# Convolution and token mixer on one core: y^T's last channels on both partition halves, a narrow identity among the first loads, the last batch's stores in halves, and a planner that knows the store queue and shifts due times by kind

## The chip, the cores and the metric

The kernel runs on one core of one Trainium2 chip. The metric is device time in microseconds for the whole program: inputs and output lie in HBM. Before the change the median of three runs is 185.41 us (185.27 to 186.28). The core has TensorE (PE, with its weight loads shown as PEld), VectorE (DVE), ScalarE (ACT), GpSimd (POOL) and SyncE (SP). Here GpSimd issues the loads of x (they convert float32 to bf16 on the way) and SyncE issues the weights' loads and all stores.

## The reference

x is 8 batches of 4,224 rows by 192 channels. First a causal convolution with 7 taps, whose weights are a softmax and are shared by the 24 channels of each of 8 heads. Then a mixer over the tokens of a batch.

```
y      = conv(x, softmax(weight))                 # per head of 24 channels, 7 taps
W_tok  = (y @ w_q) @ (y @ w_k).T / sqrt(64)       # 4224 x 4224 per batch
out    = relu(W_tok @ y) @ w_out                  # 192 x 192 output weights
```

The kernel never forms W_tok. Since W_tok y = (y w_q)(w_k^T y^T y) / 8, it computes G = y^T y (192 x 192) and M = w_k^T G (64 x 192), and then relu((y w_q) M) w_out.

## The kernel before, in words

**Tiling.** A batch is cut into 35 chunks of CW = 122 output rows (each is read as 128 input rows), and for the later steps into NSB = 5 blocks: four of 1,024 columns of y^T (two halves of 512) and one of 128. The loads of x come in groups of 18 chunks (of 9 in batch 0), whose edge chunks are separate transfers.

**Set-up.** GpSimd issues the first loads of x, then makes a wide identity (IDENTW, 128 x 128 x 4, an affine_select at L341), and ScalarE copies a narrow one (IDENT) from it (L363). VectorE computes the softmax (L349 to L373) and 14 products of the identity with tap weights (L392), TensorE adds them up (L405), ScalarE copies the sums into the banded convolution matrices (L416). ScalarE also zeroes the lower half of YTH in eight pieces (L432). SyncE issues the nine weight loads (L498) once the third group of x has landed, and nine casts on ScalarE (L503) make them bf16.

**A batch.** The functions add operations to a list, batch by batch:
- gen_conv: matmuls of two heads each (L553); the evacuation to Y goes to ScalarE or VectorE (L573).
- gen_transpose: for 8 chunks at a time, transposes of channels 0 to 127 into one PSUM bank (tr_lo, L594) and of channels 128 to 191 into another (tr_hi, L606), the second with two chunks side by side in two column halves of the array. VectorE copies the first to YTL (L616). The second needs two copies to YTH, one for each half of the partitions (L627), because YTH holds all 4,224 columns on partitions 0 to 63; partitions 64 to 127 stay zero, and so does the lower half of the weight WQH.
- gen_wq: the query projection of a block, WQL by YTL (L649) and WQH by YTH (L653), two column halves side by side, evacuated to WQT (L668).
- gen_gram: G, 6 chunks at a time, in column halves (L684), in a bank of its own.
- gen_mix_weights: G is copied (L703), transposed in part (L711), multiplied to M (L730), scaled on ScalarE (L749).
- gen_mix, for the batch before: M by WQT (L778 with row halves, L789), relu (L801, L802), the output projection (L828 with row halves, L846), evacuation to OUT (L862) and one store per block (L869; 768 KB, and 96 KB for the small block).

**What sets the order.** Planner.plan places all operations on the engines with estimated durations and latencies. Each operation has a due time vt in units of batches; among those that are ready on an engine the smallest vt wins, with STAY = 0.8 added on TensorE when an operation needs another array mode (128x128, 128x64, 64x128) than the one before. Loads have an expected landing time (op.lands), 0.26 us a chunk. The order that results is fixed: each engine runs its list in order and waits on semaphores. Seven PSUM banks are handed out by the same planner, the eighth is G's. Y and WQT have two buffers, YTL and YTH one, RT three, OUT four.

Of the kernel before, what the change touches and what calls it, by code (L numbers as in the profile page):

```python
# [14 lines left out]
class Op:  # L15
# [4 lines left out]
    def __init__(self, engines, emit, ns, needs=(), after=(), banks=0, drains=None, vt=0.0, mode=FULL, tail=0.0):  # L20
        self.engines = (engines,) if isinstance(engines, str) else tuple(engines)
        self.emit = emit

        self.ns = ns

        self.needs = [x for x in needs if x is not None]

        self.after = [x for x in after if x is not None]
        self.banks = banks

        self.drains = drains
# [8 lines left out]
        self.lands = 0.0  # L40
        Op.n += 1
        self.id = Op.n


class Planner:
# [8 lines left out]
    HOLD = 1.0  # L54

    def __init__(self, nbank, first_bank):
# [5 lines left out]
        self.bank_users = [[] for _ in range(nbank)]  # L62

# [19 lines left out]
    def plan(self):  # L83
# [9 lines left out]
        while left:  # L93
# [32 lines left out]
            free[e] = op.end  # L126
            if op.banks:
# [21 lines left out]
        return max(op.end for op in self.order)  # L149
# [66 lines left out]
def bass_lightweight_conv__then__hypermixer_token_mlp_kernel(  # L216
# [55 lines left out]
    ZERO = sbuf("zero", [128, 1], BF16)  # L272
# [4 lines left out]
    WQH = sbuf("wqh", [128, DH], BF16)  # L277
# [10 lines left out]
    YTH = sbuf("yth", [128, S], BF16)  # L288
# [17 lines left out]
    def add(*a, dma=None, **k):  # L306
        op = Op(*a, **k)
        op.dma = dma
        return planner.add(op)

    def evac_ns(cols, fast=1):
# [15 lines left out]
    one = add("DVE", lambda e, op: e.memset(IDENTW[:, :, :], 1.0), 350, vt=-9)  # L327
    zero_z = add("DVE", lambda e, op: e.memset(ZERO[:, :], 0.0), 80, vt=-8.95)
# [3 lines left out]
    zero_q = add("DVE", lambda e, op: e.memset(WQH[64:128, :], 0.0), 100, vt=-8.6)  # L332
# [6 lines left out]
    identw = add(  # L339
        "POOL",  # L340
        lambda e, op: e.affine_select(  # L341
            IDENTW[:, :, :], IDENTW[:, :, :], [[-1, 128], [0, HB]], ALU.is_equal, 0.0, base=0, channel_multiplier=1
        ),
        1600,
        needs=[one],
        vt=-3.85,
    )
# [13 lines left out]
    ident = add(  # L361
        "ACT",
        lambda e, op: e.copy(IDENT[:, :], IDENTW[:, :, 0]),  # L363
        170,
        needs=[identw],
        after=[ex],
        vt=-9,
    )
# [15 lines left out]
    band_done = []  # L384
    for f in range(2):
        fill, acc = None, None
        for k in range(KC):
            o = (f * KC + k) * CW * HB
            part = PARTS[:, o : o + CW * HB]
            made = add(  # L390
                "DVE",
                lambda e, op, part=part, k=k, f=f: e.tensor_tensor(  # L392
                    part.rearrange("p (j h) -> p j h", h=HB),
                    IDENTW[:, k : k + CW, :],
                    WSB[:, k, HB * f : HB * f + HB].unsqueeze(1).to_broadcast([128, CW, HB]),
                    ALU.mult,
                ),
                330,
                needs=[wn, identw],
                vt=-7 + f + 0.1 * k,  # L400
            )

            def collect(e, op, part=part, k=k, fill=fill):
                to = op if fill is None else fill
                return e.matmul(  # L405
                    bank(to.bank)[:, 0 : CW * HB], IDENT[:, :], part, start=k == 0, stop=k == KC - 1, skip_group_check=True
# [3 lines left out]
                "PE", collect, CW * HB / 2.4, needs=[made, ident], after=[acc], banks=1 if k == 0 else 0, vt=-7 + f + 0.1 * k  # L410
            )
            fill = fill or acc
        band_done.append(
            add(
                "ACT",
                lambda e, op, f=f, fill=fill: e.copy(  # L416
                    BAND[:, HB * f : HB * f + HB, 0:CW],
                    bank(fill.bank)[:, 0 : CW * HB].rearrange("p (j h) -> p h j", h=HB),
                ),
                56 + CW * HB / 1.2,  # L420
                needs=[acc],
                drains=fill,
                vt=-7 + f,
            )
        )
    zero_yt = []
    for i in range(8):
        n = S // 8
        zero_yt.append(
            add(  # L430
                "ACT",
                lambda e, op, i=i, n=n: e.copy(YTH[64:128, i * n : i * n + n], ZERO[64:128, 0:1].to_broadcast([64, n])),  # L432
                50 + n / 1.2,
                needs=[zero_z],
                after=band_done,
                vt=0.3 + 0.1 * i,
            )
        )
    out_first = [acc]
# [3 lines left out]
    at = [5200.0]  # L443

    def gen_load(b, gi):
# [23 lines left out]
        def emit(e, op):  # L469
            return [(e.dma_start(d, s), 16) for d, s in parts]  # L470

        at[0] += len(cs) * 260.0
        op = add(
            "POOL",
            emit,
            900 * len(parts),
            needs=[zero_x] if cs[-1] == NCC - 1 else [],
            dma=(f"x{b}_{gi}", sem, 16 * len(parts)),
            vt=-4 + b + gi * 0.1,
        )  # L480
        op.tail = 1500.0
        op.lands = at[0]
        load[b, gi] = op
# [16 lines left out]
    load_c = add("SP", emit_weights, 5000, needs=[load[0, 2]], dma=("c", S_C, 16 * 9), tail=2500, vt=-3)  # L500
# [4 lines left out]
    def twice(ap):  # L505
# [4 lines left out]
        cast(WQH[0:HI, :], WHI[0:HI, QS], [zero_q]),  # L510
# [15 lines left out]
    yt_done, yt_read, wq_read, rt_read, m_read = {}, {}, {}, {}, {}  # L526
# [11 lines left out]
    def gen_conv(b, gi):  # L538
# [6 lines left out]
        for hp in range(H // 2):  # L545
            vt = b + c0 / NCC - 0.15 + 0.02 * hp

            def conv(e, op, hp=hp):
# [15 lines left out]
                "PE", conv, mm_ns(n * GRP, 2), needs=[load[b, gi], band_done[hp // (HB // 2)], zero_b, zero_x, zero_x0], after=ev_needs, banks=nb, vt=vt  # L564
            )
# [9 lines left out]
            ev = add(both, evac, evac_ns(2 * n * GRP), needs=ev_needs, drains=mm, vt=vt)  # L575
# [3 lines left out]
    def gen_transpose(b, cs):  # L579
# [4 lines left out]
        half = (n + 1) // 2  # L584
# [12 lines left out]
        def tr_hi(e, op):  # L597
            ps = bank(op.bank).bitcast(BF16)
            last = None
            for k in range(half):  # L600
                for i in range(2):
                    if k + i * half >= n:
                        continue
                    c = cs[k + i * half]
                    w = width[c]
                    last = e.transpose(  # L606
                        ps[64 * i : 64 * i + HI, k * CW : k * CW + w], Y[0:w, yb, c, LO:D], IDENT[0:w, 0:w]
                    )
            return last

        mm_l = add("PE", tr_lo, 57 * n, needs=needs, after=free, banks=1, vt=vt)
        mm_h = add("PE", tr_hi, 57 * half, needs=needs, after=free, banks=1, vt=vt, mode=COL2)
# [4 lines left out]
                evac_ns(cols, 2), needs=free, drains=mm_l, vt=vt,  # L617
            )
        ]
        for i in range(2):  # L620
            a, z = t0 + i * half * CW, min(t1, t0 + (i + 1) * half * CW)
            if z <= a:
                continue
            evs.append(
                add(
                    "DVE",
                    lambda e, op, i=i, a=a, z=z: e.tensor_copy(  # L627
                        YTH[0:HI, a:z], bank(mm_h.bank).bitcast(BF16)[64 * i : 64 * i + HI, 0 : z - a]
                    ),
                    evac_ns(z - a, 2), needs=free, drains=mm_h, vt=vt,  # L630
                )
            )
        y_read.setdefault((b, "all"), []).extend([mm_l, mm_h])
        for c in cs:
            yt_done[b, c] = evs

    def gen_wq(b, j):
# [5 lines left out]
        wfree = wq_read.get((b - 2, j), [])  # L643

# [302 lines left out]
```

## Time and profile before

| | |
|---|---|
| Median of the runs | 185.41 us |
| Profiled execution | 185.54 us, of which 183.8 us span |
| TensorE busy | 163.0 us (89% of the span) |
| VectorE busy | 138.8 us (75%) |
| ScalarE busy | 127.5 us (69%) |
| GpSimd busy | 31.6 us (17%) |
| Bytes moved | 40.26 MB; 27.56 MB read from HBM, 25.95 MB written |

The span is that of the profiled execution, from its first to its last instruction. A group's row gives line, engine, operation, what is written from what, the count, and behind the bar busy microseconds and mean nanoseconds of one; behind the second bar the idle time before it and what ended it. TensorE's matmuls overlap, and their ends are modelled, so that the busy share is an upper bound of how full the engine is; the spacing of their starts tells more. A row of the timeline merges neighbouring instructions of one kind: start, length, engine, line, operation, and the count at the end.

### The profile page before, as it was taken

What the parts mean: (1) busy time and instruction counts of PE and PEld (TensorE: products, weight loads), DVE (VectorE), ACT (ScalarE), POOL (GpSimd) and SP (SyncE); (2) the same over time, 40 slices, a digit from 0 to 9 for tenths busy, and PEclk for the clock granted to TensorE, in tenths of its full rate; (3) what the DMA queues carried; (4) which work ended last, traced back from release to release, by engine and by line L of the source; (5) the groups of instructions that cost most, each with busy time, mean ns of one, the idle gap of its engine ahead of it and who ended that gap; (6) DMA issues with size and microseconds to landing.
All of it is one profiled execution on the core that took longest, in us unless ns stands there. A gap on an engine that the chain in (4) does not pass through costs nothing.

```text
span 183.8 us, 5487 instructions
## 1 busy us (share of the span) xinstructions
PE 163.0 (89%) x2390; PEld 108.7 (59%) x2390; DVE 138.8 (75%) x255; ACT 127.5 (69%) x220; POOL 31.6 (17%) x39
## 2 busy tenths in 40 slices
PE   0589869999999999999999999999999999979930
PEld 0248727666747575757566566677674856744520
DVE  6978868987678768877788796987679597768540
ACT  3079385778796868676784868787877786679730
POOL 7999923325030000000000000000000000000000
PEclk9999999999999999999999999999999999999996
DMA  3999999999999999999999952708442380844894
GB/s 24 182 186 189 202 193 191 191 194 192 322 288 236 266 277 294 266 277 215 335 280 282 247 213 92 277 5 341 165 170 107 126 318 25 342 175 180 328 385 180
DMA packets 47063, 40.26 MB, mean 219 GB/s; under 512 B 37568, under 2 KB 38848, under 8 KB 47040
## 3 DMA queue, kind: packets, MB, share of 16 engines
q0 software_dynamic: 36128, 13.61, 62.1%
q1 hardware_dynamic: 10912, 26.31, 38.9%
q8 instruction: 19, 0.31, 0.7%
q14 instruction: 4, 0.03, 0.0%
HBM read 27.56 MB, written 25.95 MB: 291 GB/s over the span
## 4 chain that ended last, share of the span: by engine, by line
PE 72%; DMA 7%; DVE 7%; ACT 4%; SPq 2%; POOL 2%; issue 2%; POOLq 0%
PE ps L846 15%; PE ps L684 12%; PE ps L553 9%; PE ps L828 9%; PE ps L594 7%; PE ps L649 5%; DMA xw<-in_x_dram 4%; PE ps L606 4%; PE ps L653 4%; PE ps L789 4%; PE ps L778 3%; DMA whi<-in_moe_w_out_dram 3%; SPq L498 2%; DVE rt L802 2%; DVE yth L627 2%
## 5 line engine op out<-in xcount | busy, mean ns | idle before, releaser
L862 ACT COPY out_sb<-ps 128x768 f32<-128x768 f32 (+1 forms) x43 | 33.1, 777 | 12.9 <-PE ps L846 12.3
L801 ACT ACTIVATE rt<-ps 128x1024 bf16<-128x1024 f32 (+3 forms) x49 | 33.1, 701 | 11.2 <-PE ps L778 10.7
L573 ACT CAST y<-ps 122x816 bf16<-122x816 f32 (+3 forms) x48 | 36.8, 795 | 4.7 <-PE ps L553 4.4
L862 DVE COPY out_sb<-ps 128x768 f32<-128x768 f32 (+1 forms) x29 | 24.1, 832 | 17.6 <-PE ps L846 17.5
L627 DVE COPY yth<-ps 64x488 bf16<-64x488 bf16 (+1 forms) x80 | 29.9, 374 | 6.6 <-PE ps L606 4.2
L684 PE MATMUL ps<-y 122*64 122x192 bf16 (+2 forms) x840 | 33.8, 221 | 0.4 <-issue 0.4
L470 POOL DMA_DIRECT2D xw<-in_x_dram x34 | 29.8, 904 | 22.9 <-issue 22.0
L553 PE MATMUL ps<-xw,band 128*128 128x432 bf16 (+3 forms) x144 | 30.3, 322 | 1.4 <-DVE y L573 0.5
L684 PEld LDWEIGHTS ps<-y 122*64 122x64 bf16 x840 | 28.5, 111 | 4.8 <-issue 3.8
L846 PE MATMUL ps<-wol,rt 128*128 128x192 bf16 x264 | 31.0, 251 | 0.0
L802 DVE TENSOR_SCALAR rt<-ps 128x512 bf16<-128x512 f32 (+2 forms) x31 | 25.3, 828 | 4.9 <-PE ps L789 3.7
L846 PEld LDWEIGHTS ps<-wol,rt 128*128 128x128 bf16 x264 | 21.0, 116 | 7.8 <-issue 2.1
L573 DVE CAST y<-ps 122x864 bf16<-122x864 f32 (+3 forms) x24 | 21.2, 902 | 3.3 <-PE ps L553 2.9
L616 DVE COPY ytl<-ps 128x976 bf16<-128x976 bf16 (+1 forms) x40 | 22.6, 589 | 1.2 <-PE ps L594 1.1
L828 PE MATMUL ps<-woh,rt 64*128 64x192 bf16 x264 | 21.0, 253 | 2.6 <-DVE rt L802 1.8
L594 PE MATMUL ps<-ident,y 122*128 122x122 bf16 x280 | 20.2, 216 | 1.4 <-DVE y L573 0.9
L594 PEld LDWEIGHTS ps<-ident,y 122*128 122x128 bf16 x280 | 16.8, 97 | 6.1 <-DVE y L573 1.1
L828 PEld LDWEIGHTS ps<-woh,rt 64*128 64x128 bf16 x264 | 10.4, 116 | 12.9 <-DVE rt L802 2.6
L553 PEld LDWEIGHTS ps<-xw,band 128*128 128x128 bf16 x144 | 11.6, 97 | 10.8 <-issue 2.4
L649 PE MATMUL ps<-ytl,wql 128*64 128x512 bf16 (+1 forms) x72 | 14.7, 373 | 1.3 <-ACT y L573 1.1
L606 PE MATMUL ps<-ident,y 122*64 122x122 bf16 x280 | 14.8, 217 | 0.0
L668 ACT CAST wqt<-ps 128x512 bf16<-128x512 f32 (+1 forms) x23 | 11.8, 530 | 3.7 <-PE ps L653 3.0
(64 smaller groups left out, 131.0 us busy)
## 6 DMA issues: line engine op xcount, KB each, us to landing
out_dram<-out_sb SPq DMA_DIRECT2D x32, 768.0 KB, 4.2
xw<-in_x_dram POOLq DMA_DIRECT2D x7, 816.0 KB, 33.7
xw<-in_x_dram POOLq DMA_DIRECT2D x7, 768.0 KB, 36.9
xw<-in_x_dram POOLq DMA_DIRECT2D x2, 432.0 KB, 7.1
out_dram<-out_sb SPq DMA_DIRECT2D x8, 96.0 KB, 4.3
xw<-in_x_dram POOLq DMA_DIRECT2D x1, 384.0 KB, 5.5
xw<-in_x_dram POOLq DMA_DIRECT2D x8, 45.8 KB, 22.7
xw<-in_x_dram POOLq DMA_DIRECT2D x1, 336.0 KB, 7.0
```

The source lines that it names most:

```text
L470: return [(e.dma_start(d, s), 16) for d, s in parts]
L553: last = e.matmul(PS[:, o : o + n * GRP], BAND[:, h, :], XW[:, b, c0 : c0 + n, GRP * h : GRP * h + GRP], start=True, stop=True,)
L573: return e.copy(dst, src) if op.engine == "ACT" else e.tensor_copy(dst, src)
L594: last = e.transpose(ps[:, o : o + w], Y[0:w, yb, c, 0:LO], IDENT[0:w, 0:w])
L627: lambda e, op, i=i, a=a, z=z: e.tensor_copy(YTH[0:HI, a:z], bank(mm_h.bank).bitcast(BF16)[64 * i : 64 * i + HI, 0 : z - a]),
L649: last = e.matmul(ps[64 * i : 64 * i + DH, 0:n], WQL[:, :], YTL[:, t0 + i * n : t0 + (i + 1) * n], start=True, stop=False)
L684: mm = e.matmul(bank(GB)[p : p + 64, o : o + z - r], Y[0:w, yb, c, r : r + 64], Y[0:w, yb, c, r:z], start=st, stop=end, skip_group_check=True,
L801: return e.activation(dst, src(), AF.Relu)
L802: return e.tensor_scalar(dst, src(), 0.0, None, op0=ALU.max)
L828: last = e.matmul(bank(op.bank + a)[:, o : o + D], RT[64 * a : 64 * a + HI, slot, 2, i:n:nt], WOH[64 * a : 64 * a + HI, :], start=i == q, ...
L846: last = e.matmul(bank(fh.bank + a)[:, o : o + D], RT[:, slot, a, i:n:nt], WOL[:, :], start=False, stop=True, skip_group_check=True,)
L862: return e.copy(dst, src) if op.engine == "ACT" else e.tensor_copy(dst, src)
```

## The change

- **YTH on both halves.** YTH has as many columns as WQT: a block's first 512 columns of channels 128 to 191 lie on partitions 0 to 63, its second 512 on partitions 64 to 127. The second transposes move from gen_transpose into gen_transpose_hi, called by gen_wq for each block: each half of a block transposes every chunk that it touches, into its own half of the array and of one bank, shifted so that both halves begin at the same column, and one VectorE copy takes the block over all 128 partitions. WQH becomes 128 x 2 x 64: the weight stands in rows 0 to 63 of one half and in rows 64 to 127 of the other, the rest is zero, so there is a second cast. The eight zeroings become one memset of the small block's columns.
- **Narrow identity.** GpSimd makes IDENT (128 x 128) directly after one load, that of batch 0's full chunks 1 to 8; all other loads are placed after it. Each transfer of a group is an operation of its own. ScalarE copies the wide identity from the narrow one.
- **Stores.** A block of the last batch is stored in two halves of two output tiles each, so that a run of bytes in HBM is 1,536 long in place of 3,072; each half waits for its own evacuation.
- **Planner.** It tracks when the store queue is free (op.size). Each operation has a kind, and a table of shifts (TURN) is added to its due time; without a kind the shift is -0.36. In the last batch but one the due times of the mix and output steps are lowered by another 0.36. The list of x's expected landings begins at 5.0 us in place of 5.2.

```diff
-    YTH = sbuf("yth", [128, S], BF16)
+    YTH = sbuf("yth", [128, wq_cols[-1]], BF16)
-    WQH = sbuf("wqh", [128, DH], BF16)
+    WQH = sbuf("wqh", [128, 2, DH], BF16)
...
+            if op.size:
+                self.store_free = max(op.end + 1300.0, self.store_free) + op.size / 390.0
+                op.tail = self.store_free + 700.0 - op.end
...
+    TURN = {
+        None: -0.36, "conv": -0.39, "fin_hi": 0.2, "fin_lo": -0.13, "g": -0.29, "gram": 0.01, "gt": 0.37,
+        "m": -0.33, "mix_hi": 0.08, "mix_lo": -0.01, "ms": 0.64, "out": -0.7, "rh": -0.7, "rt": 0.7,
+        "tr_hi": -0.04, "tr_lo": 0.25, "turn": 0.08, "wq": 0.02, "wqt": 0.3, "y": 0.08, "yth": 0.19,
+        "ytl": 0.7,
+    }
+        op.vt += TURN.get(kind, 0.0)
...
-    one = add("DVE", lambda e, op: e.memset(IDENTW[:, :, :], 1.0), 350, vt=-9)
+    one = add("DVE", lambda e, op: e.memset(IDENT[:, :], 1.0), 100, vt=-9.5)
+    zero_yt = add("DVE", lambda e, op: e.memset(YTH[64:128, wq_cols[-2] :], 0.0), 100, vt=-8.52)
...
+    ident = add(
         "POOL",
+            IDENT[:, :], IDENT[:, :], [[-1, 128]], ALU.is_equal, 0.0, base=0, channel_multiplier=1
...
+    identw = add(
+        "ACT",
+        lambda e, op: e.copy(IDENTW[:, :, :], IDENT[:, :].unsqueeze(2).to_broadcast([128, 128, HB])),
+        490, needs=[ident], vt=-9,
+    )
...
+            first = (b, gi) == (0, 0) and part[0].shape[1] > 1 and len(part[0].shape) == 3
+            op = add(
+                "POOL", lambda e, op, part=part: e.dma_start(*part), 900,
+                needs=[zero_x] if cs[-1] == NCC - 1 else [],
+                after=[] if first else [ident],
+                dma=(f"x{b}_{gi}", sem, 16),
+                vt=-10 if first else -4 + b + gi * 0.1 + 0.02 * k,
+            )
...
+        cast(WQH[HI:128, 1, :], WHI[HI:128, QS], [zero_q]),
...
+    def gen_transpose_hi(b, j):
+        yb = b % 2
+        t0, n, nh = SB[j]
+        parts = [chunks_in(t0 + i * n, t0 + i * n + n) for i in range(nh)]
+        lead = [t0 + i * n - parts[i][0] * CW for i in range(nh)]
+        at = max(lead)
+        q0 = wq_cols[j]
+        needs = [*{id(r): r for p in parts for c in p for r in y_done[b, c]}.values(), ident]
+        free = yth_read.get((b - 1, j), [])
+        vt = b + 0.15 + (t0 + n * nh) / S * 0.9
+        def tr_hi(e, op):
+            ps = bank(op.bank).bitcast(BF16)
+            last = None
+            for k in range(max(len(p) for p in parts)):
+                for i in range(nh):
+                    if k >= len(parts[i]):
+                        continue
+                    c = parts[i][k]
+                    w, o = width[c], at - lead[i] + (c - parts[i][0]) * CW
+                    last = e.transpose(ps[64 * i : 64 * i + HI, o : o + w], Y[0:w, yb, c, LO:D], IDENT[0:w, 0:w])
+            return last
+        mm = add("PE", tr_hi, 55 * max(len(p) for p in parts), needs=needs, after=free, banks=1, vt=vt, mode=COL2, kind="tr_hi")
+        return add(
+            "DVE",
+            lambda e, op: e.tensor_copy(
+                YTH[0 : 64 * nh, q0 : q0 + n], bank(mm.bank).bitcast(BF16)[0 : 64 * nh, at : at + n]
+            ),
+            evac_ns(n, 2), needs=[*free, zero_yt], drains=mm, vt=vt, kind="yth")
...
+                    ps[64 * i : 64 * i + DH, 0:n], WQH[:, i, :], YTH[:, q0 : q0 + n], start=False, stop=True
...
+        vt = b + 1.2 + t0 / S * 0.95 + (TURN.get(None, 0.0) if b == B - 2 else 0.0)
...
+        pieces = 2 if b == B - 1 and nt > 1 else 1
...
+            if (q + step) % (nt // pieces) == 0:
+                def emit_store(e, op, qa=q + step - nt // pieces, qz=q + step):
+                    dst = bass.AP(
+                        out_t, (b * S + t0 + qa) * D, [[nt * D, 128], [n * D, nh], [1, (qz - qa) * D]]
+                    )
+                    return e.dma_start(dst, OUT[:, oslot, 0:nh, qa:qz, :].rearrange("p t q d -> p t (q d)"))
+                store = add("SP", emit_store, 500, needs=list(outs), dma=(f"o{oslot}", S_OUT[oslot], 16), vt=fvt)
+                store.size = 128 * nh * (nt // pieces) * D * 4
```

More of the change, by code (lines that the diff above doesn't have):

```diff
@@ L40, in __init__ @@
         self.lands = 0.0
+        self.size = 0
         Op.n += 1
@@ L148, in plan @@
         assert len(self.order) == len(self.ops)
-        return max(op.end for op in self.order)
+        return max(op.end + (op.tail if op.size else 0.0) for op in self.order)
     @staticmethod
@@ L405, in collect @@
                 return e.matmul(
-                    bank(to.bank)[:, 0 : CW * HB], IDENT[:, :], part, start=k == 0, stop=k == KC - 1, skip_group_check=True
+                    bank(to.bank)[:, 0 : part.shape[1]], IDENT[:, :], part, start=k == 0, stop=k == KC - 1, skip_group_check=True
                 )
             acc = add(
-                "PE", collect, CW * HB / 2.4, needs=[made, ident], after=[acc], banks=1 if k == 0 else 0, vt=-7 + f + 0.1 * k
+                "PE", collect, CW * nh / 2.4, needs=[made, ident], after=[acc], banks=1 if k == 0 else 0, vt=made.vt
             )
             fill = fill or acc
[L413 to L424, printed above, removed]
-        )
[L426 to L439, printed above, removed]
+        done = add(
+            "ACT",
+            lambda e, op, h0=h0, nh=nh, fill=fill: e.copy(
+                BAND[:, h0 : h0 + nh, 0:CW], bank(fill.bank)[:, 0 : CW * nh].rearrange("p (j h) -> p h j", h=nh)
+            ),
+            56 + CW * nh / 1.2,
+            needs=[acc],
+            drains=fill,
+            vt=made.vt,
+        )
+        out_first.append(acc)
+        for h in range(h0, h0 + nh):
+            band_done[h] = done
     load = {}
-    at = [5200.0]
+    at = [5000.0]
     def gen_load(b, gi):
@@ L595, in tr_lo @@
             return last
[L597 to L612, printed above, removed]
+        mm_l = add("PE", tr_lo, 57 * n, needs=needs, after=free, banks=1, vt=vt, kind="tr_lo")
         evs = [
@@ L653, in wq @@
                 last = e.matmul(
-                    ps[64 * i : 64 * i + DH, 0:n], WQH[:, :], YTH[:, t0 + i * n : t0 + (i + 1) * n], start=False, stop=True
+                    ps[64 * i : 64 * i + DH, 0:n], WQH[:, i, :], YTH[:, q0 : q0 + n], start=False, stop=True
                 )
             return last
-        mq = add("PE", wq, mm_ns(n, 2), needs=[*{id(r): r for c in cs for r in yt_done[b, c]}.values(), *zero_yt, *casts],
-            after=wfree, banks=1, vt=vt, mode=COL2)
+        mq = add("PE", wq, mm_ns(n, 2), needs=[*{id(r): r for c in cs for r in yt_done[b, c]}.values(), turned, *casts],
+            after=wfree, banks=1, vt=vt, mode=COL2, kind="wq")
+        yth_read[b, j] = [mq]
         for c in cs:
@@ L692, in gram @@
             return mm
-        a = add("PE", gram, 84 * len(cs), needs=[*needs, *before], after=begun, vt=vt, mode=COL2)
+        a = add("PE", gram, 84 * len(cs), needs=[*needs, *before], after=begun, vt=vt, mode=COL2, kind="gram")
         y_read.setdefault((b, "all"), []).append(a)
@@ L838, in gen_mix @@
             fvt = vt + 0.05 + 0.02 * q
-            fh = add("PE", fin_hi, mm_ns(D, step), needs=[rl, rh, *casts], after=ofree, banks=nh, vt=fvt, mode=ROW2)
+            fh = add("PE", fin_hi, mm_ns(D, step), needs=[rl, rh, *casts], after=ofree, banks=nh, vt=fvt, mode=ROW2, kind="fin_hi")
             def fin_lo(e, op, iq=iq, q=q, fh=fh):
```

144 lines of the change are left out of this document (55 added, 89 removed).

## The prediction

> **What bounds the kernel now.** I read the page first, then busy time by stretches, then the chain that ended last, the waits of TensorE's weight loads, the groups by shape, and the timeline of a steady batch and of the end.
>
> ```profile
> span 183.8 us, 5487 instructions
> PE 163.0 (89%) x2390; PEld 108.7 (59%) x2390; DVE 138.8 (75%) x255; ACT 127.5 (69%) x220; POOL 31.6 (17%) x39
> GB/s 24 182 186 189 202 193 191 191 194 192 322 288 236 266 277 294 266 277 215 335 280 282 247 213 92 277 5 341 165 170 107 126 318 25 342 175 180 328 385 180
> ...
> 10.40:26.50 16.10, 12.52 (x220) 9.79 (x220) 12.76 (x27) 12.16 (x29) 12.89 (x16) 1.00 1.56 193
> 26.50:160.00 133.50, 132.30 (x2014) 88.91 (x2016) 105.94 (x185) 99.57 (x166) 9.48 (x11) 1.00 1.02 225
> 160.00:178.00 18.00, 14.51 (x152) 8.73 (x148) 11.56 (x17) 13.34 (x23) 0.00 (x0) 1.00 0.69 263
> ```
>
> The profiled execution took 185.54 us, its span 183.8, so 1.7 us lie around the span; the median of the runs is 185.41, 0.13 less. In the rows of the stretches the busy times stand in the order PE, PEld, DVE, ACT, POOL. From 26.5 to 160 us TensorE is busy 132.3 of 133.5 us by the records, VectorE 79% and ScalarE 75%: TensorE sets the pace there. Before 26.5 and after 160 it does not. The start is a chain of transfers:
>
> ```profile
> 5.54 7.15 DMA xw<-in_x_dram
> ...
> 17.24 6.17 DMA whi<-in_moe_w_out_dram
> 25.08 0.35 ACT wol L503
> 26.52 0.41 PE ps L649 x2
> ```
>
> The third group of x lands at 12.69; only then does SP issue nine weight loads, the last of which lands at 23.41; nine casts on ScalarE follow, one evacuation, and the first query projection at 26.52. Whatever of batch 0 is done sooner before that waits for it.
>
> The pace between is read from the transpose of G, once a batch:
>
> ```profile
> L711 PE MATMUL ps<-ident,gsb x8: 219/219/229, 24.2 to 161.0; 128*128 128x128 bf16 x8
> ```
>
> (161.0 − 24.2) / 7 = 19.5 us a batch.
>
> **Start (identity, loads).** The changed POOL queue is: x's full chunks 1 to 8, the narrow select, then all other loads.
>
> ```profile
> 3.96 1.62 POOL L341 TENSOR_SCALAR_AFFINE_SELECT identw<-identw 128x512 bf16<-128x512 bf16 x1
> 4.72 0.89 DVE L370 TENSOR_SCALAR wsm<-wsm 128x8 f32<-128x8 f32 x1
> 6.16 4.61 DVE L392 TENSOR_TENSOR out_sb<-identw,wsb 128x488 bf16<-128x488 bf16 x14
> L470 POOL DMA_DIRECT2D xw<-in_x_dram x34: 545/952/1360, 1.3 to 54.3; - x34
> L432 ACT COPY yth<-zero 64x528 bf16<-64x528 bf16 x8 | 4.5, 624 | 0.1
> L503 ACT CAST wqh<-whi 64x64 bf16<-64x64 f32 x1 | 0.2, 240 | 0.0
> ```
>
> One load (0.95 us from 1.3) ends at 2.25. The select of a quarter of the elements takes between a quarter of 1.62 and all of it, so it ends at 2.65 to 3.9. Three more issues follow, so the third x group is issued by 5.5 to 6.7, where now its issue begins at 5.54 and ends at 6.5. Its bytes queue behind two earlier groups at about 190 GB/s in either case, so its landing moves by −0.5 to +0.2; I take 0, since the one load that runs ahead can run dry before the next is issued. Every load of the first batch passes the select on POOL; all later ones only follow in the old order.
>
> The tiny VectorE steps for the softmax end when L392 starts, at 6.16; L370, eight elements wide, takes 0.89 us and ends 0.03 us after the select does, and the select will be gone by then, so the band may be ready some 0.7 us earlier. On ScalarE the wide copy of the identity (estimate 0.6, from 64x528 in 0.62) stands ahead of the exponential, which may be 0.2 late for it. Neither counts: the weights' landing at 23.41 covers both. If that cover were gone they would be worth −0.7 and +0.2. The eight zeroings (4.5 us of ScalarE between 12 and 19 us) go at nothing under the same cover. The second cast of WQH lies on the path: +0.24. Start: **+0.2**.
>
> **Transposes of the last 64 channels.**
>
> ```profile
> L606 PE MATMUL ps<-ident,y 122*64 122x122 bf16 x272 | 14.8, 217 | 0.0
> 66.44 0.38 PE L606 MATMUL ps<-ident,y 122*64 122x122 bf16 x7
> 66.75 0.52 PE L828 MATMUL ps<-woh,rt 64*128 64x192 bf16 x8
> ```
>
> They are now made per 1,024-column block, and a chunk that straddles an edge is transposed twice. Chunks of 122 in halves of 512: 5+5, 5+5, 5+6, 5+5, and 2 for the last 128 columns, 43 a batch against 35. Two run side by side: seven take 0.38 us, of which the last one's own 0.217 are no spacing, so (0.38 − 0.217) / 6 = 27 ns each and 54 ns a pair. Pair steps go from 4+4+4+4+2 = 18 to 5+5+6+5+2 = 23. Five more by 54 ns is 0.27 us a batch, seven batches in the stretch that TensorE bounds: **+1.9**. The projection's matmuls stay as many and as wide; the weight's zero half now lies in WQH.
>
> **VectorE's copies.**
>
> ```profile
> L627 DVE COPY yth<-ps 64x488 bf16<-64x488 bf16 x64 | 26.1, 408 | 5.5 <-PE ps L606 3.5
> L627 DVE COPY yth<-ps 64x244 bf16<-64x244 bf16 x8 | 2.2, 273 | 0.8 <-PE ps L606 0.7
> L627 DVE COPY yth<-ps 64x76 bf16<-64x76 bf16 x8 | 1.6, 199 | 0.2
> L616 DVE COPY ytl<-ps 128x976 bf16<-128x976 bf16 x32 | 20.7, 657 | 1.2 <-PE ps L594 1.1
> L616 DVE COPY ytl<-ps 128x320 bf16<-128x320 bf16 x8 | 2.5, 314 | 0.0
> ```
>
> Now 80 copies, 26.1 + 2.2 + 1.6 = 29.9 us. Afterwards four of 128x512 and one of 64x128 a batch. By the ytl rows a column costs (657 − 314) / 656 = 0.52 ns, so 512 columns take 314 + 192 × 0.52 = 0.41 us; 128 columns lie between 0.20 and 0.27, take 0.22. Eight batches: 8 × (4 × 0.41 + 0.22) = 15.0 us. VectorE loses **14.9 us** of work, 13 of them in the steady stretch. It is not on the path there; what it can give back is TensorE's waiting:
>
> ```profile
> PEld ps L649 <- DVE yth L627: 2.1, 5, 0.5
> ...
> PEld ps L789 <- DVE y L573: 0.2, 1, 0.2
> ```
>
> These are the first and last of 30 rows of weight-load waits between 26.5 and 160 us that end at ScalarE or VectorE; together 17.7 us, 4.7 of them at this copy. A weight load runs about one matmul ahead, so a wait is partly under streaming. I take half of the 4.7 (the copy still exists, half as often), 12% of the other 13.0 (13 us less of 205.5 us of evacuations is 6%, and queueing counts it about twice), that is 2.4 + 1.6, and three quarters of it as real: **−3.0**. Bounds: nothing (all of it hidden by the 99% busy PE) and −8 (every wait at VectorE and some at ScalarE).
>
> **New order.** The offsets by kind put convolutions 0.39 of a batch (7.6 us) ahead, first transposes 0.25 behind, output copies first in the evacuation queues. What that can win on TensorE is changes of array mode:
>
> ```profile
> 61.83 0.22 PE L730 MATMUL ps<-gsb,wkl 128*128 128x128 bf16 x1
> ...
> 79.50 0.58 PE L684 MATMUL ps<-y 122*64 122x64 bf16 x14
> ```
>
> From the first to the last of these 62 rows the mode changes 19 times, about 20 a batch. One costs 66.75 − 66.44 − 7 × 0.027 = 0.12 us, the gap between the last transposes and L828. So 17 us of the seven batches are changes. Two fewer a batch are worth 1.7 us: **−1.7**. The transposes now stand beside the projection in the same mode, which favours fewer; bounds are three more a batch (+2.5) and five fewer (−4.2).
>
> **End.**
>
> ```profile
> 162.19 16.20 SPq L869 DMA_DIRECT2D out_dram<-out_sb  x9
> 176.13 2.26 SPq L869 DMA_DIRECT2D out_dram<-out_sb  x2
> 176.99 0.96 DVE out_sb L862
> out_dram<-out_sb SPq DMA_DIRECT2D x32, 768.0 KB, 4.2
> ```
>
> The last copy ends at 177.95, the last store is issued by 178.39, and the span ends 5.4 us later; 786 kB at the page's 385 GB/s (174.6 to 179.2) are 2.0 of these. A half leaves 1.0 us less behind the last copy. Against it stand packets of 1,536 bytes in place of 3,072. Loads with 384-byte packets ran at 190 GB/s; a straight line in time per packet between 190 and 385 gives 335 at 1,536 bytes, so 3.15 MB of the last batch would take 1.2 us longer if the queue never ran dry. Between −1.0 and +0.4, and since the queue is full only in the last slices: **−0.6**. The four more issues on SP are 0.4 us each with nothing behind them but stores; each half waits for its own copy alone. The Trainium skill ("DMA: Bandwidth & Descriptors", section "Why small descriptors are slow (HBM only)") puts a fixed cost of about 3 cycles on each packet of 32-byte beats: two of 51 against one of 99 is 3%, an estimate of 0.25 us over the last batch, by which the halves would give −0.8; no run here shows 1,536-byte packets.
>
> Nine stores are issued from 162.19 on, five of them the last batch's, four still the one before. The change takes 0.36 of a batch off that batch's due times, so these four come before the last G. From 160 to 178 TensorE idles 18.0 − 14.5 = 3.5 us; the work pulled ahead pushes G back by its own length, so only idle time can be won. I take a bit over a third: **−1.3**, bounds 0 and −3.5.
>
> **Sum.** +0.2 + 1.9 − 3.0 − 1.7 − 0.6 − 1.3 = −4.5; 185.54 − 4.5 = 181.0, and 0.13 less by the median: **180.9 us**.
>
> **Rivals.** *TensorE hides the relief.* It is 99% busy, the waits lie under streaming, and the order wins no changes of mode. Then +0.2 + 1.9 − 0.6 − 1.3 leaves 185.6: no difference. For it: PE's own idle time in the steady stretch is only 1.2 us. Against: the 17.7 us of load waits. Chance 0.10.
>
> *Convolutions stand ahead of their data.* Batch 2's convolutions, at 33.9 and 44.1 us now, would be placed some 7.6 us sooner, and TensorE takes its queue in order: everything behind them waits.
>
> ```profile
> 33.88 0.89 PE ps L553 x4
> 44.21 0.36 PE ps L553 x2
> ```
>
> Batches 0, 1 and 2 (each some 35 chunks of 128x192 bf16, 1.70 MB) at about 190 GB/s from 5 us on, with 0.3 MB of weights, end at 5 + 5.4/0.19 = 33 us or later, so the second half of batch 2 is due near 34.5. The code expects it at 32.3 (5.0 plus 0.26 a chunk, 105 chunks). Two halves late by 2.2 us each are +4.4; with rival one's other terms and the relief lost in it, 190.0. It decides only if both are placed right at the expected landing. From batch 3 on loads lead by more than the shift. Chance 0.10.
>
> *The order wins more.* Five fewer changes a batch and twice the relief: 180.9 − 2.5 − 3.0 = 175.4. Chance 0.12. That the change fails to do what it says I give no chance of its own: each half has its own semaphore count and pieces.
>
> **How the numbers follow.** The forecast has 0.68. A measurement here can tell about 0.5% from no change, 0.9 us. The range takes in the forecast with its terms' bounds, most of the third rival and the first: 176.0 to 186.0. Faster: 0.68 and 0.12 (0.80); same: 0.10; slower: 0.10.
>
> **What would show it.** L627's successor: 40 copies, four of five near 0.41 us, VectorE's total near 124 us. The transposes: 344 in place of 280. G's pace: 19.5 down to about 19.1. Weight-load waits at VectorE and ScalarE near 13 us. Last copy to the end of the span: 4.8 us in place of 5.85. First projection still at 26 to 27 us. Wrong if the pace stays at 19.5 or above, if TensorE waits for x in its second or third batch, or if the store queue runs full past the last copy.

## The result and the profile after

The kernel after takes 178.32 us in the median of four runs (177.82 to 178.53), the kernel before, timed beside it, 185.34 (185.11 to 186.28): a ratio of 0.961, 95% interval 0.957 to 0.965. The profiled execution fell from 185.54 to 178.53 us and its span from 183.8 to 176.8. Forecast were 180.9 us; the direction was right and the gain was 7.0 us in place of 4.5.

The page of after, and its busy time by stretches (columns: stretch, length, then PE, PEld, DVE, ACT, POOL busy, granted clock, DMA share, GB/s):

```profile
span 176.8 us, 5567 instructions
PE 161.5 (91%) x2454; PEld 112.3 (64%) x2454; DVE 123.5 (70%) x219; ACT 122.6 (69%) x209; POOL 30.3 (17%) x39
```

```profile
26.50:155.00 128.50, 128.38 (x2049) 91.13 (x2047) 92.17 (x152) 97.35 (x159) 9.23 (x11) 1.00 1.05 231
155.00:171.00 16.00, 15.22 (x163) 9.02 (x160) 11.27 (x18) 12.80 (x21) 0.00 (x0) 1.00 0.72 281
```

VectorE lost 138.8 - 123.5 = 15.3 us, near the 14.9 worked out from the rows. TensorE is still the engine that is busy nearly all the time, and now up to 171 us too (15.22 of 16.00 us).

The groups of after that stand for the moved transposes and their copies, and the transpose of G:

```profile
L633 PE MATMUL ps<-ident,y 122*64 122x122 bf16 x336 | 16.8, 217 | 0.0
L640 DVE COPY yth<-ps 128x512 bf16<-128x512 bf16 x32 | 13.5, 421 | 5.2 <-PE ps L633 4.8
L640 DVE COPY yth<-ps 64x128 bf16<-64x128 bf16 x8 | 1.6, 206 | 0.3 <-PE ps L633 0.3
...
L633 PE MATMUL ps<-ident,y 76*64 76x76 bf16 x8 | 1.6, 199 | 0.0
```

```profile
L720 PE MATMUL ps<-ident,gsb x8: 219/219/230, 24.1 to 156.4; 128*128 128x128 bf16 x8
```

344 transposes, 40 copies, 0.42 and 0.21 us each: the counts and prices that were forecast. The pace is (156.4 - 24.1) / 7 = 18.9 us a batch, against 19.5 before and about 19.1 forecast.

The chain at the start, and the waits of TensorE's weight loads between 26.5 and 155 us that end at ScalarE or VectorE (first and last of 17 rows, 6.6 us together; before has 17.7 in 30 rows between 26.5 and 160 us, 17.4 of them up to 155):

```profile
1.31 1.01 POOL xw L479
2.40 0.31 POOL ident L359
2.71 1.50 POOL xw L479 x2
4.21 8.96 DMA xw<-in_x_dram
...
17.72 5.80 DMA whi<-in_moe_w_out_dram
...
26.24 0.41 PE ps L658 x2
```

```profile
PEld ps L658 <- DVE ytl L605: 1.1, 3, 0.4
...
PEld ps L835 <- ACT mbd L755: 0.2, 1, 0.2
```

The third group of x lands at 13.17, the weights at 23.52, the first projection starts at 26.24 (before 26.52). The end, by the issues of stores after the last G, and the last copy on ScalarE:

```profile
157.47 6.10 SPq L877 DMA_DIRECT2D out_dram<-out_sb  x4
```

```profile
166.50 7.08 SPq L877 DMA_DIRECT2D out_dram<-out_sb  x9
```

```profile
172.43 0.32 ACT out_sb L869
```

The first row is the four stores of batch 6 that are issued after the last G; the second the eight halves and the small store of batch 7. The last copy ends at 172.75 and the span 4.05 us later.

So the 7.0 us lie as follows. Up to the first projection: 0.3. From there to the last G: 161.0 - 26.52 = 134.5 us before, 156.4 - 26.24 = 130.2 after, 4.3 less. From the last G to the last copy: 177.95 - 161.0 = 16.9 before, 16.4 after, 0.6 less (with rounding). From the last copy to the end: 5.85 before, 4.05 after, 1.8 less; the section on the hardware takes this last part up.

### The profile page after: what moved, and what is told of

Same layout as the page of the kernel before. It is cut to its first block, busy times and chain, and to the rows that moved or that the text cites. A ratio compares the mean times of both kernels' runs of the same rounds, so it can differ in the third digit from the quotient of the medians.

```text
span 176.8 us, 5567 instructions
## 1 busy us (share of the span) xinstructions
PE 161.5 (91%) x2454; PEld 112.3 (64%) x2454; DVE 123.5 (70%) x219; ACT 122.6 (69%) x209; POOL 30.3 (17%) x39
## 3 DMA queue, kind: packets, MB, share of 16 engines
q0 software_dynamic: 36128, 13.61, 64.7%
HBM read 27.56 MB, written 25.95 MB: 303 GB/s over the span
## 4 chain that ended last, share of the span: by engine, by line
PE 81%; DMA 8%; ACT 3%; SPq 2%; POOL 2%; issue 1%; POOLq 0%
PE ps L853 15%; PE ps L694 14%; PE ps L559 11%; PE ps L835 9%; PE ps L598 7%; DMA xw<-in_x_dram 5%; PE ps L633 5%; PE ps L784 5%; PE ps L658 5%; PE ps L795 5%; PE ps L662 4%; DMA whi<-in_moe_w_out_dram 3%; SPq L503 2%; POOL xw L479 1%; ACT out_sb L869 1%
## 5 line engine op out<-in xcount | busy, mean ns | idle before, releaser
L869 DVE COPY out_sb<-ps 128x768 f32<-128x768 f32 (+1 forms) x36 | 32.0, 891 | 25.4 <-PE ps L853 25.3
L807 ACT ACTIVATE rt<-ps 128x1024 bf16<-128x1024 f32 (+3 forms) x50 | 37.9, 770 | 14.0 <-PE ps L784 13.4
L578 ACT CAST y<-ps 122x864 bf16<-122x864 f32 (+3 forms) x49 | 36.9, 793 | 8.1 <-PE ps L559 7.6
L869 ACT COPY out_sb<-ps 128x768 f32<-128x768 f32 (+1 forms) x36 | 26.6, 746 | 10.7 <-PE ps L853 10.2
L694 PE MATMUL ps<-y 122*64 122x128 bf16 (+2 forms) x840 | 34.0, 222 | 0.0
L559 PE MATMUL ps<-xw,band 128*128 128x432 bf16 (+3 forms) x144 | 31.4, 323 | 0.8 <-ACT band L433 0.7
L578 DVE CAST y<-ps 122x816 bf16<-122x816 f32 (+3 forms) x23 | 20.6, 912 | 3.9 <-PE ps L559 3.6
L808 DVE TENSOR_SCALAR rt<-ps 128x512 bf16<-128x512 f32 (+3 forms) x30 | 20.1, 681 | 4.7 <-PE ps L784 2.7
L640 DVE COPY yth<-ps 128x512 bf16<-128x512 bf16 (+1 forms) x40 | 14.9, 378 | 5.5 <-PE ps L633 5.1
L633 PE MATMUL ps<-ident,y 122*64 122x122 bf16 (+1 forms) x344 | 17.0, 217 | 0.0
L658 PE MATMUL ps<-ytl,wql 128*64 128x512 bf16 (+1 forms) x72 | 14.6, 368 | 1.9 <-ACT woh L508 1.9
```

The lines of the kernel that those rows point to most:

```text
L559: last = e.matmul(PS[:, o : o + n * GRP], BAND[:, h, :], XW[:, b, c0 : c0 + n, GRP * h : GRP * h + GRP], start=True, stop=True,)
L578: return e.copy(dst, src) if op.engine == "ACT" else e.tensor_copy(dst, src)
L633: last = e.transpose(ps[64 * i : 64 * i + HI, o : o + w], Y[0:w, yb, c, LO:D], IDENT[0:w, 0:w])
L658: last = e.matmul(ps[64 * i : 64 * i + DH, 0:n], WQL[:, :], YTL[:, t0 + i * n : t0 + (i + 1) * n], start=True, stop=False)
L694: mm = e.matmul(bank(GB)[p : p + 64, o : o + z - r], Y[0:w, yb, c, r : r + 64], Y[0:w, yb, c, r:z], start=st, stop=end, skip_group_check=True,
L807: return e.activation(dst, src(), AF.Relu)
```

## The experiments

Three readings stood against each other: that the terms of the prediction are right one by one; that TensorE hides VectorE's relief and only the order wins; and that the order pays only together with the new layout. Medians below are to be read against 185.3 to 185.4 for before in the same batch of runs and 178.3 for after. Where the text says that the order was kept, every engine runs the same list of operations as its parent and only what one of them does was changed; elsewhere the planner laid out a new order. A profile shows one execution of a kernel. In the executions of runs 4, 6 and 7, which start as after does, the first projection stands at 25.4 to 25.7 us, where after's stands at 26.24; so a start scatters by up to 0.8 us from one trace to the next.

**1. The layout alone.** Before, with the second transposes per block, YTH and WQH on both halves and the one memset:

```diff
-    YTH = sbuf("yth", [128, S], BF16)
+    YTH = sbuf("yth", [128, wq_cols[-1]], BF16)
-    WQH = sbuf("wqh", [128, DH], BF16)
+    WQH = sbuf("wqh", [128, 2, DH], BF16)
+    def gen_transpose_hi(b, j):
...
```

> Before, with the last channels of y^T on both halves alone (second transposes per block, wide WQH, one memset for eight zeroings); due times, identity, loads and stores as before. By the prediction's terms +1.9 for 64 more transposes and -3.0 for VectorE's relief: about 184.3 us, pace of G 19.3 us a batch. If TensorE hides the relief: 187.2 or a little more, pace 19.8. If relief is worth what the whole change won: 179 or below. VectorE near 124 us in each case.

182.5 us, ratio 0.985 (0.984 to 0.987): 2.8 us gained, more than the two terms' 1.1.

```profile
L703 PE MATMUL ps<-ident,gsb x8: 219/219/230, 25.6 to 161.5; 128*128 128x128 bf16 x8
```

```profile
175.35 0.80 ACT out_sb L854
```

The last G stands at 161.5, no earlier than before (161.0); the whole gain is behind it. The last copy ends at 176.15, 1.8 us earlier than before, and the span ends 5.1 us later in place of 5.85. Counting, over all matmuls of a trace, where the rows and columns of the array in use differ from the matmul before, the array changes its mode 165 times before, 148 times here and 152 times after. At the prediction's 0.12 us the 17 fewer are an estimated 2.0 us. They were counted in the prediction under the new order; they come with the layout.

**2. The planner's part alone** (the shifts by kind, the last batch but one's extra shift and the store queue's estimate), on the old layout with whole stores:

```diff
+        op.vt += TURN.get(kind, 0.0)
...
+        vt = b + 1.2 + t0 / S * 0.95 + (TURN.get(None, 0.0) if b == B - 2 else 0.0)
```

> Before, with the planner's part alone: shifts of due times by kind, the last batch but one's extra shift, the store queue's estimate; old layout of y^T, whole stores. By the prediction's terms -1.7 and -1.3: about 182.4. If the relief is hidden and the order alone wins: 178 or below (all of the gain, without the 1.9 of added transposes). If the order pays only once VectorE is relieved: 185 or above, since the shifts were laid out for another set of operations.

183.7 us, ratio 0.992 (0.991 to 0.994): 1.5 us gained, between the cases. It changes the array's mode 166 times, no less often than before. The waits of the weight loads at ScalarE and VectorE up to 155 us fall from 17.4 to 9.2 us. The last copy ends at 175.28, 2.7 us earlier than before:

```profile
174.32 0.96 DVE out_sb L877
```

**3. Everything but the shifts.**

```diff
-    TURN = {
...
-    }
+    TURN = {}
```

> After, with every shift of due times at zero (the extra one of the last batch but one with them): layout, identity, loads and halves stay. By the prediction's terms 185.4 + 0.2 + 1.9 - 3.0 - 0.6 = 183.9. If the relief is hidden: 186.9. If the order is worth nothing on top of the layout: 178.3, as after.

183.4 us, ratio 0.991 (0.990 to 0.993), near the 183.9 of the terms. On the new layout the shifts are worth 183.4 - 178.3 = 5.1 us; on the old one the planner's part is worth 1.5. The parts do not add up: 2.8 from the layout and 1.5 from the planner make 4.3, the whole is 7.0, and what else was changed is worth next to nothing (runs 4 and 10). The profiles show where the rest lies. By the spans the layout gains 2.5 us, the planner 2.1 and the whole 7.0, so that 2.4 are missing. Up to the last copy the two gain 1.8 and 2.7, and the whole 5.2: 0.7 are missing there. The other 1.7 lie behind the last copy, where the stores drain (5.85 us before, 5.1 in run 1, 6.4 in run 2, 4.05 in after). In run 3 the last copy ends at 176.92:

```profile
175.96 0.96 DVE out_sb L864
```

That is 4.2 us behind after's, so up to the last copy the shifts are worth 4.2 us here, and the planner's part 2.7 on the old layout. The profiled execution of run 3 took 182.37 us, 1.0 less than the median, so this is one trace against another and no more.

**4. Whole stores in the last batch.**

```diff
-        pieces = 2 if b == B - 1 and nt > 1 else 1
+        pieces = 1
```

> After, with the last batch stored in whole blocks. By the prediction's term 178.3 + 0.6 = 178.9. By the rate that the trace of after shows for packets of 1,536 bytes (no slower than 3,072) the full 1.0 us: 179.3, and the last copy to the end of the span 5 us or more in place of 4.05. If the queue were only shifted: 178.3.

178.4 us, ratio 0.964 (0.962 to 0.967): 0.1 us, not to be told from nothing. The stretch in which the last batch is stored, first of after, then of this kernel:

```profile
168.00:175.00 7.00, 3.84 (x38) 2.12 (x35) 2.93 (x4) 3.42 (x6) 0.00 (x0) 0.95 1.07 400
```

```profile
168.00:175.00 7.00, 3.33 (x33) 1.95 (x31) 2.23 (x4) 2.71 (x5) 0.00 (x0) 0.91 1.03 416
```

Both move bytes without a gap for the whole 7 us, past the last copy: the queue is full, so a smaller last piece only shifts what is waited for. In these two stretches runs of 1,536 bytes go at 400 GB/s and of 3,072 at 416; before's own stores of 3,072 bytes go at 388 between 173 and 180 us, so no price of the shorter runs can be read from this.

**5. VectorE's relief at the old order.** Before, order kept, the copies to YTH 16 columns wide from the second batch on:

```diff
-                    lambda e, op, i=i, a=a, z=z: e.tensor_copy(
+                    lambda e, op, i=i, a=a, z=z if b == 0 else a + 16: e.tensor_copy(
```

> Before, every engine's order kept, with the copies to YTH 16 columns wide from the second batch on (the rest of YTH keeps the first batch's values, so part of the copying is left out): VectorE loses some 14 to 16 us, TensorE nothing. By the prediction's term for VectorE's relief 185.3 - 3.0 = 182.3. If TensorE hides the relief in a fixed order: 185.3.

```profile
PE 159.2 (88%) x2372; PEld 109.2 (60%) x2390; DVE 124.2 (69%) x255; ACT 127.3 (70%) x220; POOL 31.6 (17%) x39
```

183.3 us, ratio 0.988 (0.986 to 0.990): VectorE's 14.6 us less are worth 2.1. TensorE's matmuls stand in the same order and the waits of its weight loads fell from 17.7 to 12.3 us, so that here some 40% of the waiting that went was time.

**6. VectorE's old load at the new order.** After, order kept, each block's copy made as two:

```diff
-            lambda e, op: e.tensor_copy(
-                YTH[0 : 64 * nh, q0 : q0 + n], bank(mm.bank).bitcast(BF16)[0 : 64 * nh, at : at + n]
-            ),
+            lambda e, op: [e.tensor_copy(
+                YTH[64 * i : 64 * i + 64, q0 : q0 + n], bank(mm.bank).bitcast(BF16)[64 * i : 64 * i + 64, at : at + n]
+            ) for i in range(nh)][-1],
```

> After, order kept, with each block's copy to YTH made as two of 64 partitions, so that VectorE has its old load (some 13 us more). If VectorE's load is what lets the new order pay: 181.3 or above. If TensorE hides it: 178.3 to 178.8.

```profile
PE 161.5 (90%) x2433; PEld 112.2 (63%) x2454; DVE 137.1 (76%) x251; ACT 122.9 (69%) x209; POOL 30.3 (17%) x39
```

181.1 us, ratio 0.977 (0.975 to 0.979): 13.6 us more on VectorE cost 2.8, a little under the case that the load decides. With the fifth run this settles the first rival: TensorE does not hide the relief, in either order. The waits of the weight loads rose only from 6.6 to 8.9 us (up to 155 us), less than the time that was lost, so their sum has no fixed price.

**7. The added transposes once more.** After, order kept, the first pair of each block made twice:

```diff
-            for k in range(max(len(p) for p in parts)):
+            for k in [0, *range(max(len(p) for p in parts))]:
```

> After, order kept, with the first pair of each block's second transposes made twice: 5 pair steps more a batch, 40 in all, as many as the change added. By the prediction's 54 ns a step, seven batches on the path: 178.3 + 1.9 = 180.2. If the added transposes hide under waits: 178.3.

```profile
L720 PE MATMUL ps<-ident,gsb x8: 219/219/230, 24.2 to 157.6; 128*128 128x128 bf16 x8
```

```profile
173.63 0.32 ACT out_sb L869
```

181.1 us, ratio 0.977 (0.974 to 0.980): 2.7 more, above both cases. The last G and the last copy are only 1.2 us later than in after; another 1.4 us lie between the last copy and the end (5.4 in place of 4.05), which the section on the hardware takes up. The first projection stands 0.5 us earlier in this trace (25.74), so that from there to the last copy the steps cost 1.7: on TensorE's path they cost 1.2 to 1.7.

**8. Convolutions at their old due time.**

```diff
-        None: -0.36, "conv": -0.39, "fin_hi": 0.2, "fin_lo": -0.13, "g": -0.29, "gram": 0.01, "gt": 0.37,
+        None: -0.36, "conv": 0.0, "fin_hi": 0.2, "fin_lo": -0.13, "g": -0.29, "gram": 0.01, "gt": 0.37,
```

> After, with the shift of the convolutions' due times at zero in place of -0.39, all else as after. If the earlier convolutions are what the shifts win: 181 or above, towards the 183.4 without shifts. If they are one of many: 178.5 to 179.5. If early convolutions cost waits for x (the prediction's rival): below 178.

180.8 us, ratio 0.974 (0.971 to 0.977): 2.5 us lost, between the first two cases, though the modes change as often (153 times). In the profile the last copy ends 1.5 us later than in after, and another 1.1 us lie behind it (5.15 us to the end). So early convolutions win, some 1.5 us up to the last copy, and in after they wait for no x. Of the prediction's rival not a row is seen in TensorE's waits over the whole span of after, the start's apart:

```profile
PE ps L658 <- ACT woh L508: 1.9, 1, 1.9
PE ps L835 <- ACT rt L807: 0.7, 2, 0.4
PE ps L559 <- ACT band L433: 0.7, 1, 0.7
PE ps L598 <- DVE y L578: 0.4, 1, 0.4
PE ps L720 <- DVE gsb L713: 0.3, 1, 0.3
PE ps L835 <- ACT out_sb L869: 0.2, 1, 0.2
```

**9. The weights sooner.** After, order kept; SP waits for the first group of x in place of the third:

```diff
-    planner.plan()
+    planner.plan(); load_c.needs = list(load[0, 0])
```

> After, every engine's order kept, but SP issues the nine weight loads when the first group of x has landed (6.8 us in the trace of after) in place of the third (13.2 us). If the weights' landing bounds the start, as the prediction has it, the casts begin some 1.6 us sooner (ScalarE is free at 21.95, the weights now land at 23.53), the first projection stands at 24.6 in place of 26.2, and the whole is 176.7 to 177.3. If x's later groups are delayed by as much, or TensorE makes the time up later: 178.3.

The casts and the first projection's wait in this kernel, on ScalarE and TensorE:

```profile
22.02 0.25 ACT L508 CAST wql<-wlo 128x64 bf16<-128x64 f32 x1
...
24.71 0.41 PE L658 MATMUL ps<-ytl,wql 128*64 128x512 bf16 x2 [0.20 <-ACT woh L508]
```

```profile
L720 PE MATMUL ps<-ident,gsb x8: 219/220/229, 24.3 to 154.8; 128*128 128x128 bf16 x8
```

177.4 us, ratio 0.956 (0.955 to 0.958), the shortest time here and 0.1 above the range expected; its interval overlaps that of after (0.957 to 0.965) by 0.001. The first projection moved by 1.5 us and the last G by 1.6; the span is 1.4 us shorter, the median 0.9. Against the 25.4 to 25.7 of runs 4, 6 and 7 the first projection moved by 0.7 to 1.0. The start's bound is the weights' landing, as the prediction read it.

**10. The old identity and loads.**

```diff
-            IDENT[:, :], IDENT[:, :], [[-1, 128]], ALU.is_equal, 0.0, base=0, channel_multiplier=1
+            IDENTW[:, :, :], IDENTW[:, :, :], [[-1, 128], [0, HB]], ALU.is_equal, 0.0, base=0, channel_multiplier=1
...
-                vt=-10 if first else -4 + b + gi * 0.1 + 0.02 * k,
+            vt=-4 + b + gi * 0.1,
```

> After, TensorE's order kept, with the wide identity made on GpSimd behind three loads, the narrow one copied from it, and the loads in their old order. By the prediction's working the weights' landing covers all of it: 178.3. If the earlier band counts for the end: 178.8 to 179.2.

178.7 us, ratio 0.964 (0.962 to 0.965): within the noise of after. The narrow identity is covered, as forecast.

**11. Without the last batch but one's extra shift.**

```diff
-        vt = b + 1.2 + t0 / S * 0.95 + (TURN.get(None, 0.0) if b == B - 2 else 0.0)
+        vt = b + 1.2 + t0 / S * 0.95
```

> After, without the extra -0.36 on the mix and output steps of the last batch but one; orders differ at the end only. By the prediction's term 178.3 + 1.3 = 179.6, with the last batch's G earlier and a longer way from G to the last copy than 16.4 us. If the shift is worth nothing, since the work pulled ahead pushes G back by its length: 178.3.

```profile
L720 PE MATMUL ps<-ident,gsb x8: 219/220/230, 24.2 to 152.3; 128*128 128x128 bf16 x8
```

```profile
172.25 0.32 ACT out_sb L869
```

179.9 us, ratio 0.970 (0.968 to 0.972): 1.6 us lost, near the 1.3 forecast. G is 4.1 us earlier, and yet the last copy ends at 172.57 where after's ends at 172.75; the work that was not done before G is done behind it (20.3 us from G to the last copy, 16.4 in after). The loss itself stands behind the last copy: 5.3 us to the end in place of 4.05. So the time is near the forecast and the way is not: what the extra shift won is in the drain of the stores, and not idle time of TensorE.

**12. Half of every shift.**

```diff
-        op.vt += TURN.get(kind, 0.0)
+        op.vt += 0.5 * TURN.get(kind, 0.0)
```

> After, with every shift of due times at half its value. If the shifts win by their direction (convolutions early, first transposes late, output copies first), half of them keeps most of the 5.1 us between 183.4 (none) and 178.3 (all): 179 to 181. If the gain belongs to this one arrangement of operations: 182 to 184.5, no better than none.

```profile
L720 PE MATMUL ps<-ident,gsb x8: 218/220/230, 24.7 to 164.3; 128*128 128x128 bf16 x8
```

183.1 us, ratio 0.989 (0.985 to 0.993), as slow as without shifts. The last G is at 164.3, the latest of all. Yet the array changes its mode 147 times and the weight loads wait 9.6 us at ScalarE and VectorE (26.5 to 155 us), both less than without shifts (152 times, 14.2 us). So neither the changes of mode nor these waits say what an order costs. The gain belongs to one arrangement of operations, not to a direction that half a step would share.

## Why the prediction was right, and where it was off

*What bounds the kernel* held. TensorE sets the pace, the start is a chain of transfers, and the end is a queue of stores.

*Start, +0.2.* Right to the noise. The first projection is 0.3 us earlier, not later; the old identity and loads (run 10) change nothing at the end, and what does (run 9) is the landing of the weights. The select took 0.31 us, less than the quarter of 1.62 (0.41) that the prediction took as the least.

*Transposes, +1.9.* As many again cost 1.2 us by the place of the last copy and 1.7 from the first projection to it (run 7): the term was near, perhaps a little high.

*VectorE's relief, -3.0.* Measured 2.1 at the old order and 2.8 at the new one. The mechanism was right and the size nearly. At the old order the waits of the weight loads fell by 5.4 us, where 4.0 were forecast, and "three quarters of it as real" was too high for them (2.1 us). In after 6.6 us of waits are left, where some 13 were forecast, since the order cut them as well.

*New order, -1.7.* This is the term that was mis-sized, and its mechanism did not hold. It was priced by changes of array mode alone, two fewer a batch. The count came out (13 fewer in all, an estimated 1.6 us), but by luck: the fewer changes came with the layout (run 1), and the shifts win 5.1 us on top of it while they change the mode as often as no shifts do (152 times in both). The prediction had put the waits of the weight loads wholly down to VectorE's load; the shifts cut them too, from 14.2 us in run 3 to 6.6 in after. But the waits do not account for the gain either: on the old layout the planner's part cut them by 8.2 us for 1.5 us of time (run 2), and half of every shift cut them by 4.6 us for nothing (run 12). That this order wins is shown, and that moving the convolutions back loses part of it (run 8); by what it wins was not found out. The prediction also gave the order one price, where runs 2 and 3 have 1.5 and 5.1 us. Up to the last copy the difference is smaller: 2.7 us on the old layout, 3.4 to 4.2 on the new one (against runs 1 and 3). So the order suits the new layout somewhat better, why is open, and the rest of the difference lies in how the stores drain and in the scatter from one execution to the next.

*End: halves, -0.6.* Measured 0.1, within noise. The step that failed is "the queue is full only in the last slices": it is full from 168 us to past the last copy, which the prediction itself had named as a sign of being wrong. The cost worked out beside it was off as well, 335 GB/s on a straight line against 400. One end of that line was the loads of x at 190 GB/s, but these convert float32 to bf16, so that 190 GB/s written are 380 read (13.61 MB on their queue, 27.56 MB read from HBM by the whole program): they are transfers of another kind. The Trainium skill ("DMA: Bandwidth & Descriptors", section "Why small descriptors are slow (HBM only)") gave 3% for the smaller packets, as the prediction worked out from it. That is nearer to the 400 measured than the line through the rows, but the stores of 3,072 bytes scatter from 388 (before) to 416 GB/s (run 4), and no run here can tell 3% from nothing.

*End: order, -1.3.* 1.6 measured (run 11), but that the sizes agree is luck. "these four come before the last G" failed: four stores of batch 6 still follow it, in after as before. "only idle time can be won" failed too: run 11 without the shift reaches its last copy as early and loses the time behind it.

*Hardly in the sum*: the stretch from the last copy to the end became 1.8 us shorter, where the prediction had 1.0, all of it by the halves. They explain 0.35 at most (4.4 us in run 4, 4.05 in after). The rest goes with a trickle at the end of the stores, which before has and after has not; the section on the hardware shows it.

*The rivals.* TensorE hiding the relief fell with runs 5 and 6; convolutions ahead of their data with the waits of after. The third, that the order wins more, came about in its size by nearly half (178.3 lies between the forecast and its 175.4), but not by its mechanism: there were not five fewer changes a batch, and VectorE's relief was worth no more than forecast.

## What to carry to other kernels

Where an order is laid out by a planner, run a change of layout and a change of order each alone and both, and keep the order fixed when the price of one operation is asked. Compare the traces up to the last copy and behind it separately: here most of what did not add up lay behind it. Weight-load waits on the busiest engine are worth looking at even where its records show it 99% busy, but their sum is no price: 5.4 us less of them gained 2.1 us in one run, 2.3 more cost 2.8 in another, and a third had 4.6 less and gained nothing. Before splitting the last transfers, look whether the queue is full past the last copy: then the size of the last piece hardly counts.

## What the runs showed of the hardware

**Fetches of the program and the last stores.** The views of the DMA queues in the last stretch, by fortieths of it, first of before (160 to 183.8 us), then of after (165 to 176.8), of run 7 (168 to 180) and of run 11 (165 to 177.9):

```profile
GB/s 399 84 0 0 0 364 394 379 174 0 0 0 0 364 394 379 360 398 399 379 113 159 399 389 399 410 399 364 394 399 391 318 405 399 392 161 26 26 5 0
...
q8 instruction: 2, 0.03, 0.5%
```

```profile
GB/s 448 375 427 115 10 56 0 0 318 391 396 386 411 396 391 391 417 406 391 396 391 412 406 396 396 391 411 406 380 411 391 412 396 391 391 310 23 0 0 0
...
q8 instruction: 1, 0.02, 0.5%
```

```profile
GB/s 0 20 374 394 399 394 404 410 400 394 399 384 374 434 384 379 389 374 379 404 394 400 405 410 394 394 399 399 361 100 26 26 20 26 23 3 0 0 0 0
...
q8 instruction: 1, 0.02, 0.6%
```

```profile
GB/s 400 441 400 400 364 296 331 391 405 391 419 386 257 410 410 391 391 410 405 395 386 400 419 395 381 405 419 391 386 405 400 307 36 24 24 24 24 5 0 0
...
q8 instruction: 1, 0.02, 0.4%
```

Each last stretch has a transfer of 16 KB on the queue named instruction (before's has two, and the second is meant); it takes 0.88 to 1.08 us. In before it comes at 178.1, in run 7 at 171.9 and in run 11 at 165.4, and from there on the stores move without a pause. All three end in a trickle of some 24 to 26 GB/s, about a sixteenth of the rate ahead of it (400 / 16 = 25), as if one of the 16 DMA engines were late. In after the transfer comes at 166.5, the stores pause behind it for 0.9 us, and the trickle is one slice of 0.3 us.

By the times of the packets all fourteen kernels divide in this way. In six (before, runs 2, 5, 7, 8 and 11) the stores do not pause after the last such transfer; they end in a trickle of 1.3 to 1.7 us, and 5.15 to 6.44 us lie between the last copy and the end. In the other eight (after and runs 1, 3, 4, 6, 9, 10 and 12) the stores pause for 0.45 to 2.65 us in all; the trickle is 0.3 us at most, and 3.70 to 5.11 us lie behind the last copy. So it looks as if a fetch of the program puts one engine behind, and a later pause lets it catch up. That is read from these rows; no run moved the fetch by itself.

**GpSimd's select and a long step on VectorE.** In before a tensor_scalar of eight elements took 0.89 us and ended 0.03 us after the select. In after, with the select long over at 2.71, it takes 0.35:

```profile
4.85 0.35 DVE L388 TENSOR_SCALAR wsm<-wsm 128x8 f32<-128x8 f32 x1
```

The Trainium skill ("SBUF — State Buffer", section "Who interferes with whom") says that such an instruction, if it runs in a two-port mode, waits for a GpSimd instruction that was issued first. The trace agrees, with 0.54 us here, though no view shows the mode. In run 10, whose select is as wide as before's, a step with two inputs meets it:

```profile
3.97 1.60 POOL L359 TENSOR_SCALAR_AFFINE_SELECT identw<-identw 128x512 bf16<-128x512 bf16 x1
...
4.30 1.20 DVE L373 TENSOR_TENSOR wex<-wt_f,wmx 128x56 f32<-128x56 f32 x1
```

It begins after the select and takes 1.20 us. In before it began 0.01 us ahead of the select and took 0.22.
